# Attention and a mixture of experts on one core: some k loads leave the planner's estimate of transfers, and GpSimd's chores may follow each other after four steps, not five

## The chip, the cores and the metric

The kernel runs on one core of a Trainium2 chip. The metric is the device time of one execution in microseconds (us). The time before is the median of three runs. A profile of one execution stands beside them, with a trace of every instruction. Engines are named as in the profile: PE is TensorE's matmul, PEld its weight load, DVE is VectorE, ACT is ScalarE, POOL is GpSimd, SP is SyncE. A name with a small q behind it (SPq) is an engine's own queue of waits and DMA issues.

## The reference

Two blocks follow each other. The first is a lightning attention: for 4 batches and 8 heads, 768 positions of 64 channels, with a decay per head, and a state of 64 x 64 that is carried from block to block. Its output is laid out as 3072 tokens of 512 channels. The second is a mixture of four experts, each of two matrices with a ReLU between them, weighted by normalised probabilities.

```python
def _attn_ref(q, k, v, lam):            # q, k, v: (4, 8, 768, 64), block = 64
    ...
    for b in range(nb):
        sl = slice(b * block, (b + 1) * block)
        qb, kb, vb = (q[:, :, sl], k[:, :, sl], v[:, :, sl])
        intra = np.einsum('bhic,bhjc->bhij', qb, kb) * Dmask[None]
        intra = np.einsum('bhij,bhjd->bhid', intra, vb)
        inter = np.einsum('bhid,bhde->bhie', qb * lam_pow[None], kv_state)
        out[:, :, sl] = intra + inter
        kb_dec = kb * rev_pow[None]
        kv_state = lam_block[None, :, None, None] * kv_state + np.einsum('bhsd,bhse->bhde', kb_dec, vb)

def _moe_ref(x, domain_probs, w1, w2):  # x: (3072, 512), w1: (4, 512, 1024), w2: (4, 1024, 512)
    p = domain_probs / (domain_probs.sum(-1, keepdims=True) + 1e-09)
    for e in range(E):
        h = np.maximum(x @ w1[e], 0.0)
        out += p[:, e:e + 1] * (h @ w2[e])
```

All numbers are float32.

## The kernel before

**Tiling.** The 3072 tokens form three groups of 1024, and a group with one expert is a *unit*: twelve units, numbered 0 to 11. The products are done by a Strassen scheme with seven products (M1 to M7) in place of eight. For the products with the first weights (from unit 1 on), and from unit 5 on (`NEST`) for those with the second weights too, the scheme is nested: seven inner products in each of the seven. The operands of the nested products are sums and differences of weight blocks, called S1 to S4. They are made once on GpSimd, stored in device memory (`w1_ops`, `w2_ops`), and loaded from there again and again.

**The loop.** The main loop runs over the units (`at`), over the seven products (`i`), and over the eight entries of `order` (`x`). Each entry issues a few matmuls of the second product of this unit (L1234, from unit 5 on L1551) and of the first product of the next unit (L1175). One entry is a *step*; the planner's clock `now` goes up by one with each, so a unit has 56 steps. The order in which the program is written is the order in which every engine runs it; nothing is reordered later.

**Attention beside it.** Group 0's attention comes first. Groups 1 and 2 need 16 chunks of attention (n = 8 to 23), which run between the matmuls of units 0 to 4 at steps written out by hand (`AT`). From chunk 13 on (`comes_across`), q and k reach their transposed form through device memory and transposes on VectorE, and the untransposed k is loaded by itself, one DMA of 256 KB, in `load` (L174). GpSimd multiplies that k by the decay (`decayed`), and TensorE reads the product in `scores` (L761, L768) seven steps later.

**Weight loads.** `feed` (first weights, tile `ws_in`) and `feed3` (second weights in the nested form, tile `w2t`) load one product ahead, that is eight steps. Where the operands that they read were made by GpSimd, they call `until`, which forces chores out until the store of that operand has been issued. All of these loads, and nearly all stores, are issued by SyncE, in order.

**The planner.** GpSimd's preparations wait in a list, `chores`. After each step `pump` may hand out the first of them. It keeps estimates, in steps: `busy` (when GpSimd will be done), `moved` (when the transfers issued so far will have passed), `asked` (when SyncE will have issued them) and `free` (before which no further chore is begun). `send` is the helper that issues a DMA and adds it to the estimates:

```python
n = 4 * min(packet(out), packet(in_))
moved[0] = max(moved[0], now[0]) + 4 * math.prod(out.shape) / n * (9 + n / 25) / 16 / 1714
if by is None:
    asked[0] = max(asked[0], now[0]) + 0.27
```

A chore begins only if `free` has passed, `moved` and `asked` lie less than four steps ahead (`FULL`), and, from unit 4 on, GpSimd is not booked beyond the next step. Stores of what GpSimd made wait in `queue` until their estimated time, or until a chore begins, and are then issued. From unit 5 on (`spare` is set), at least five steps pass between two chores as long as more than 13 are left, and seven after that. In a chore of `prepare_w2_ops`, `ready` makes four inner operands by four subtractions (`inner_w2`) and books their store; `total` makes one of the sums S1, S2, S4. From unit 5 on it is second weights that are prepared in this way, M3 of expert 0 among them, which unit 7 needs for its second product.

Of the kernel before, what the change touches and what calls it, by code (L numbers as in the profile page):

```python
# [21 lines left out]
def kernel(  # L22
# [30 lines left out]
    nc = tc.nc  # L53

    B, H, S, D = q.shape
# [45 lines left out]
    def packet(ap):  # L101
        n, step = 1, 1
        for stride, size in reversed(ap.ap[1:]):
            if stride != step or size == 1 and stride != 1:
                break
            n, step = n * size, step * size
        return n

    def send(out, in_, by=None):
# [4 lines that stand above are left out]
        (by or nc.sync).dma_start(out=out, in_=in_)  # L114
# [13 lines left out]
    now, busy, free, filled, moved, asked, spare = [0], [0.0], [0.0], [0.0], [0.0], [0.0], []  # L128
# [21 lines left out]
    def where(n):  # L150
        g, x = divmod(n, CPG)
        return (x // 4, x % 4) if g == 0 else (2 * g + x // 2 % 2, 2 * (x // 4) + x % 2)
# [7 lines left out]
    def load(n, names="qkv"):  # L160

        c, b = where(n)
        for name in names:
            x = ({"k": acc_tile, "v": w2_tile} if n < CPG else {}).get(name, small)(f"{name}n")
            src = {"q": q, "k": k, "v": v}[name][b, :, c * C:(c + 1) * C, :]
            if name == "v":
                to, of = x[:].rearrange("p (h d) -> p h d", d=D), src.rearrange("h p d -> p h d")
                for h in (slice(0, 4), slice(4, 8)) if n < CPG else (slice(0, 8),):
                    send(out=to[:, h], in_=of[:, h], by=nc.scalar if n == 0 and h.start else None)
            else:  # L170
                to, of = x[:].rearrange("p (i r d) -> p i r d", r=2, d=D), src.rearrange("(r i) p d -> p i r d", r=2)
                if comes_across(n):
                    to = x[:].rearrange("p (r i d) -> p i r d", r=2, d=D)
                    send(out=x[:].rearrange("p (h d) -> p h d", d=D), in_=src.rearrange("h p d -> p h d"))  # L174
                else:
                    for r in range(2):
                        by = nc.scalar if n == 0 and r == 1 else nc.sync
                        by.dma_start(out=to[:, :, r], in_=of[:, :, r])
                nat[n, name] = to
                continue  # L180
            nat[n, name] = x[:].rearrange("p (h d) -> p h d", d=D)
# [13 lines left out]
    chores, queue, late, results, made = [], [], [], [], set()  # L195
# [8 lines left out]
    def all_added(still=None):  # L204
        while adds and (still is None or adds[0][0] < still):
            adds.pop(0)[1]()

    def pump(pace=1.0, force=False):
        all_added(None if force else now[0])
        while results:  # L210
            results.pop(0)()
        while late and (force or late[0][0] <= now[0]):
            late.pop(0)[1]()
        begins = chores and (
            force or free[0] <= now[0] and max(moved[0], asked[0]) < now[0] + FULL and not resting[0]
            and not (packed and busy[0] > now[0] + 1)
        )
        while queue and (force or queue[0][0] <= now[0] or begins and len(queue) > LEFT):
            queue.pop(0)[1]()
        if begins:  # L220
            begin = free[0] = max(free[0], now[0] - 1)
            was = max(busy[0], now[0])
            chores.pop(0)()
            free[0] = max(free[0], begin + max(pace * (busy[0] - was), (5 if len(chores) > 13 else 7) if spare else 1))

    def pause(n):
        def step():
# [4 lines left out]
    def until(what):  # L232
        while what not in made:
            pump(force=True)
# [271 lines left out]
    def comes_across(n):  # L506
        return n >= FIRST_ACROSS
# [11 lines left out]
    def load_more(n):  # L519
        if not comes_across(n):  # L520
            load(n, "qk")
        else:
            trickle(sum(x <= rank[where(n)[1]] for x, _ in pieces))
            load_across(n)
            load(n, "k")

    first = small("zeros")
    zeros = first[:, 0:P]
    nc.vector.memset(zeros, 0.0)
    load(0)  # L530
    load(1)
    raw_w1(0, "A11", 0)
# [32 lines left out]
    for r in range(2):  # L565
        for ac in range(NHP):
            h = 4 * r + ac
            nc.vector.tensor_tensor_scan(
                out=s_decay[:, r, ac], data0=lam_bc[:, h:h + 1].to_broadcast([P, BL]), data1=blk_ident,
# [10 lines left out]
    for ac in range(NHP):  # L580
        nc.vector.tensor_tensor_scan(
            out=q_decay[:, ac], data0=lam_q[:, ac:ac + 1].to_broadcast([P, BL]), data1=zeros[:, 0:BL],
# [549 lines left out]
    def first_product(g, e, m, blocks, tags):  # L1132

        while (g, e, m) not in fed:
            pump(force=True)
# [635 lines left out]
    for f in (  # L1771
        (ts[0], lambda: warm(2)), (ss[0],), (ts[1], lambda: warm(1)), (vs[0], loads(4, 5)), (ss[1], loads("A21", 6)),
        (vs[1], loads("A22", 7)), (ts[2],), (m1[0],), (ss[2],), (m1[2],),
        (vs[2],), (ts[3],), (h2[0][0],), (ss[3],), (ts[4],), (h2[0][1],),
        (vs[3],), (h2[2][0],), (ss[4],), (ts[5],), (h2[2][1], sum_first("S3", "A11", "A21")),
        (vs[4],), (h1[1][0],), (ss[5],), (ts[6], sum_first("S1", "A21", "A22", ALU.add)), (h1[1][1],),
        (vs[5],), (h1[3][0],), (ss[6],), (ts[7], load_probs), (h1[3][1], sum_first("S2", "S1", "A11")),
        (vs[6],), (h2[1][0], sum_x(0)), (ss[7],), (h2[1][1], sum_first("S4", "A12", "S2")),
        (begin_chores, m2[3]), (vs[7],), (sum_x(1), quarter_5(0)), (quarter_5(2),),
    ):  # L1780
        for work in f:
            work()
        now[0] += 1
        pump()
# [66 lines left out]
    for at, (g, e) in enumerate(units):  # L1851
# [14 lines left out]
        for i in range(7):  # L1866
# [8 lines left out]
            if nests and i == 2:  # L1875
                nc.scalar.dma_start(
                    out=gate_bc, in_=gate_rows[ahead[0] - 1, :, ahead[1]].partition_broadcast(P),
# [121 lines left out]
```

## Time and profile before

| | us |
|---|---|
| median of three runs | 1152.47 |
| the three runs | 1149.34, 1152.47, 1153.88 |
| the profiled execution | 1149.36 |
| its span, from first to last instruction | 1147.6 |
| TensorE busy in the span | 1134.2 |
| VectorE, GpSimd, ScalarE busy | 765.9, 762.9, 381.4 |

The mean clock that TensorE was granted is 0.996 of full speed. The profile's page gives shares, the costliest groups and the DMA issues; further views give the waits of an engine, the chain of work that ended last, the instructions in order of time, and stretches of the span with the busy time of each engine. A busy time of PE counts matmuls whose ends are modelled. A wait is put down to what came last.

### The profile page before, as it was taken

Reading aid. Unit: us, or ns where it says so; the run is one execution under the profiler, and the core shown is the slowest. Engines: PE = TensorE matmul, PEld = TensorE weight load, DVE = VectorE, ACT = ScalarE, POOL = GpSimd, SP = SyncE. Lnnn points to the kernel's source line nnn. Section 1 sums busy time; section 2 is a strip of 40 time slices with the busy share of each in tenths; the row PEclk is TensorE's granted clock in tenths of the full one; section 3 lists DMA queues with packets and bytes.
Section 4 is the critical chain, followed back from the end, with each engine's and each line's share of the span. In section 5 each row is a group of like instructions: output and inputs, shape, how many; then the busy total and the mean of one; then the engine's idle time right before and its main releaser. Section 6 shows DMA issues by size and latency. Waiting matters only on the chain.

```text
span 1147.6 us, 22118 instructions
## 1 busy us (share of the span) xinstructions
PE 1134.2 (99%) x7991; PEld 990.9 (86%) x7991; DVE 765.9 (67%) x1472; ACT 381.4 (33%) x770; POOL 762.9 (66%) x730
## 2 busy tenths in 40 slices
PE   8999999999999999999999999989999999999998
PEld 7888888888888888888888888868888888888887
DVE  4576776587577658737665576758767566776785
ACT  3425123112212311322353443344345442342332
POOL 2738148555743697547676995994896983873885
PEclk9999999999999999999999999989999999999999
DMA  8786888899789999778558677975669767657552
GB/s 199 176 276 190 204 230 256 280 327 297 244 284 311 289 296 307 246 235 297 176 174 266 208 249 222 298 253 182 189 205 291 227 192 200 194 162 211 174 193 74
DMA packets 322748, 266.34 MB, mean 232 GB/s; under 512 B 150160, under 2 KB 266064, under 8 KB 322640
## 3 DMA queue, kind: packets, MB, share of 16 engines
q1 hardware_dynamic: 287440, 257.61, 72.5%
q10 hardware_dynamic: 35168, 7.31, 3.5%
q8 instruction: 64, 1.05, 0.4%
q14 instruction: 44, 0.36, 0.1%
q0 software_dynamic: 32, 0.00, 0.0%
HBM read 197.19 MB, written 73.43 MB: 236 GB/s over the span
## 4 chain that ended last, share of the span: by engine, by line
PE 97%; DVE 1%; DMA 1%; issue 0%; ACT 0%; SPq 0%; DVEq 0%; POOLq 0%; ACTq 0%
PE pg L1175 41%; PE pq L1551 25%; PE q L1234 21%; PE pM L1693 2%; PE pc L1693 2%; PE op L824 1%; PE sp L761 1%; PE op L842 1%; PE sp L768 1%; PE pM L1418 1%; PE pg L1551 1%; PE qp L727 1%; PE kp L727 0%; DMA w2t<-w_ops 0%; DMA decay<-in_lam_dram 0%
## 5 line engine op out<-in xcount | busy, mean ns | idle before, releaser
L1175 PE MATMUL pg<-xs,ws_in 128*128 128x256 f32 x1960 | 471.2, 380 | 0.1
L1175 PEld LDWEIGHTS pg<-xs,ws_in 128*128 128x128 f32 x1960 | 372.1, 190 | 53.2 <-DVE m L117 2.5
L117 DVE TENSOR_TENSOR m<-pg,m 128x512 f32<-128x512 f32 x374 | 255.6, 686 | 93.1 <-PE pg L1175 81.0
L1234 PE MATMUL q<-w2t,m 128*128 128x256 f32 x1120 | 265.5, 380 | 0.0
L1234 PEld LDWEIGHTS q<-w2t,m 128*128 128x128 f32 x1120 | 211.7, 190 | 29.0
L117 DVE TENSOR_TENSOR sums<-pq,sums 128x256 f32<-128x256 f32 x272 | 113.2, 421 | 98.5 <-PE pq L1551 85.8
L1551 PE MATMUL pq<-acc,w2t 128*128 128x256 f32 x688 | 170.1, 380 | 0.0
L117 POOL TENSOR_TENSOR m<-m,decay 128x512 f32<-128x512 f32 x91 | 114.2, 1273 | 79.5 <-ACT m L1192 56.4
L1551 PEld LDWEIGHTS pq<-acc,w2t 128*128 128x128 f32 x688 | 131.2, 191 | 18.2
L1192 ACT ACTIVATE m<-m 128x512 f32<-128x512 f32 x99 | 62.4, 630 | 191.3 <-DVE m L117 191.1
L1252 DVE SCALAR_TENSOR_TENSOR acc<-q,gate,acc 128x256 f32<-128x256 f32 x108 | 52.1, 483 | 80.5 <-PE q L1234 79.7
L1188 ACT COPY m<-pg 128x512 f32<-128x512 f32 x88 | 51.6, 586 | 130.9 <-PE pg L1175 115.4
L117 DVE TENSOR_TENSOR m<-m,m 128x512 f32<-128x512 f32 x108 | 88.0, 815 | 6.5 <-ACT m L1158 6.5
L117 POOL TENSOR_TENSOR acc<-hT,hT 128x512 f32<-128x512 f32 x56 | 70.4, 1272 | 22.1 <-PE pq L1551 13.6
L1152 ACT COPY pg<-m 128x512 f32<-128x512 f32 x77 | 45.4, 590 | 110.8 <-DVE m L117 103.6
L117 POOL TENSOR_TENSOR acc<-hT,acc 128x512 f32<-128x512 f32 x56 | 71.2, 1271 | 7.3 <-PE pq L1551 3.6
L1551 PE MATMUL pq<-hT,w2t 128*128 128x256 f32 x288 | 70.0, 379 | 0.0
L117 POOL TENSOR_TENSOR kn<-kn,decay 128x512 f32<-128x512 f32 x16 | 18.4, 1148 | 65.2 <-DMA kn<-in_k_dram 31.3
L1551 PE MATMUL pq<-m,w2t 128*128 128x256 f32 x228 | 56.4, 384 | 5.2 <-DMA w2t<-w_ops 5.2
L1551 PEld LDWEIGHTS pq<-hT,w2t 128*128 128x128 f32 x288 | 54.7, 190 | 7.4
L117 POOL TENSOR_TENSOR w2o<-w2b 128x512 f32<-128x512 f32 x26 | 33.7, 1319 | 41.2 <-DMA w2b<-in_moe_w_dram 36.6
L1156 ACT COPY m<-pg 128x512 f32<-128x512 f32 x44 | 25.8, 586 | 91.0 <-PE pg L1175 85.1
(157 smaller groups left out, 1457.1 us busy)
## 6 DMA issues: line engine op xcount, KB each, us to landing
ws_in<-w_ops SPq DMA_DIRECT2D x40, 512.0 KB, 4.7
w2t<-w_ops SPq DMA_DIRECT2D x72, 256.0 KB, 3.1
ws_in<-w_ops SPq DMA_DIRECT2D x60, 256.0 KB, 3.7
ws_in<-w_ops SPq DMA_DIRECT2D x40, 384.0 KB, 4.2
w2b<-in_moe_w_dram SPq DMA_DIRECT2D x56, 256.0 KB, 5.3
w_ops<-ops SPq DMA_DIRECT2D x28, 512.0 KB, 5.0
w_ops<-ops SPq DMA_DIRECT2D x54, 256.0 KB, 4.0
w2t<-w_ops SPq DMA_DIRECT2D x100, 128.0 KB, 2.9
```

Source lines behind the costliest of these rows:

```text
L117: eng.tensor_tensor(out=o, in0=a, in1=b, op=op)
L727: nc.tensor.transpose(out=x[:, ac * C:(ac + 1) * C], in_=y[:, ac].rearrange("p r d -> p (r d)"), identity=ident[:],)
L761: nc.tensor.matmul(out=sp[r][half[x], ac * BL:(ac + 1) * BL], lhsT=hc(kT)[half[r], ac, blk[x]], rhs=hc(qT)[half[r], ac, blk[x]], start=(ac ...
L1152: nc.scalar.copy(out=banks[tags[1]][:], in_=new["11"][:])
L1156: nc.scalar.copy(out=o[:], in_=p[:])
L1175: nc.tensor.matmul(out=p[:, j * 256:(j + 1) * 256], lhsT=ws[i][:, j * P:(j + 1) * P], rhs=xs[i], start=(fresh and j == 0), stop=True, skip ...
L1188: nc.scalar.copy(out=new[at][:], in_=p[:])
L1192: nc.scalar.activation(out=new[at][:], in_=new[at][:], func=AF.Relu)
L1234: nc.tensor.matmul(out=p[:, s * DH:(s + 1) * DH], lhsT=h[A_OF[m]][:, c * 256 + s * P:c * 256 + (s + 1) * P], rhs=fed2[g, e, m][uu][:, c], ...
L1252: nc.vector.scalar_tensor_tensor(out=o, in0=x, scalar=w, in1=o, op0=ALU.mult, op1=ALU.add)
L1551: nc.tensor.matmul(out=p[:, 0:256], lhsT=fed3[e, m, i][:, c * P:(c + 1) * P], rhs=b[B_OF[i]][:, c * 256:(c + 1) * 256], start=(fresh and c ...
L1693: nc.tensor.matmul(out=p[:, s * 256:(s + 1) * 256], lhsT=a[c][:, f:f + P], rhs=b[:, c, j * 256:(j + 1) * 256], start=(s == 0 and c == 0 an ...
```

## The change

There are two edits, both in the planner. In `load`, the k of a chunk from 13 on is no longer issued through `send` but by a plain DMA on SyncE, with the same source and the same target: the transfer stays as it is, and `moved` and `asked` do not count it. In `pump`, the least distance between two chores from unit 5 on, while over 13 are left, is four steps instead of five.

```diff
@@ -171,7 +171,7 @@ in load
                 if comes_across(n):
                     to = x[:].rearrange("p (r i d) -> p i r d", r=2, d=D)
-                    send(out=x[:].rearrange("p (h d) -> p h d", d=D), in_=src.rearrange("h p d -> p h d"))
+                    nc.sync.dma_start(out=x[:].rearrange("p (h d) -> p h d", d=D), in_=src.rearrange("h p d -> p h d"))
@@ -221,7 +221,7 @@ in pump
             chores.pop(0)()
-            free[0] = max(free[0], begin + max(pace * (busy[0] - was), (5 if len(chores) > 13 else 7) if spare else 1))
+            free[0] = max(free[0], begin + max(pace * (busy[0] - was), (4 if len(chores) > 13 else 7) if spare else 1))
```

## The prediction

> **What bounds the kernel now.** I read the page first: the share of each engine and the chain that ended last. Busy time, share of the span, instructions; then the chain by engine.
>
> ```profile
> span 1147.6 us, 22118 instructions
> PE 1134.2 (99%) x7991; PEld 990.9 (86%) x7991; DVE 765.9 (67%) x1472; ACT 381.4 (33%) x770; POOL 762.9 (66%) x730
> ...
> PE 97%; DVE 1%; DMA 1%; issue 0%; ACT 0%; SPq 0%; DVEq 0%; POOLq 0%; ACTq 0%
> ```
>
> TensorE is the bound, and the change touches none of its work. So the question is only where TensorE waits. The view of its waits names them all:
>
> ```profile
> PE pq L1551 <- DMA w2t<-w_ops: 5.2, 1, 5.2
> PE sp L768 <- issue: 1.4, 1, 1.4
> PE op L824 <- ACT kv L784: 1.1, 2, 1.0
> ...
> PE sp L768 <- POOL kd L117: 0.3, 1, 0.3
> ```
>
> One wait stands out: 5.2 us, once, for a load of second weights (w2t). The stretches show what it costs. Rows are from:to, length, then busy time and count of PE, PEld, DVE, ACT, POOL, the granted clock, the DMA share and GB/s; the first two are stretches of chunk work in units 1 to 4, and the next four are units 6 to 9.
>
> ```profile
> 284.00:382.50 98.50, 98.50 (x887) 86.31 (x878) 66.60 (x129) 22.64 (x51) 48.28 (x54) 1.00 0.90 281
> 382.50:481.00 98.50, 98.50 (x897) 86.32 (x896) 68.46 (x125) 23.33 (x52) 74.02 (x84) 1.00 0.93 291
> ...
> 664.30:749.30 85.00, 84.94 (x393) 74.31 (x393) 62.23 (x122) 32.95 (x61) 70.14 (x68) 1.00 0.81 255
> 749.30:842.30 93.00, 87.77 (x393) 76.34 (x393) 67.11 (x133) 35.24 (x64) 69.65 (x62) 0.96 0.64 205
> 842.30:927.00 84.70, 84.70 (x393) 74.36 (x393) 53.22 (x94) 41.71 (x86) 71.41 (x65) 1.00 0.80 249
> 927.00:1011.70 84.70, 84.70 (x393) 74.42 (x393) 60.08 (x113) 29.67 (x54) 55.22 (x45) 1.00 0.64 187
> ...
> 763.10:768.40 5.30, 0.08 (x1) 0.03 (x1) 0.50 (x1) 1.08 (x2) 5.22 (x5) 0.90 0.92 280
> 768.40:774.90 6.50, 6.50 (x17) 5.26 (x18) 2.04 (x4) 0.59 (x1) 4.79 (x5) 0.56 1.08 365
> ```
>
> Units 6 to 9 have 393 matmuls each, and TensorE is dense in three of them: 84.70 us in units 8 and 9, 85.00 in unit 6. Unit 7 takes 93.00, so 93.00 - 84.70 = 8.30 us are lost in it. The last two rows split that: TensorE stands still for 5.2 us, and then works for 6.5 us at a mean granted clock of 0.56. The chain in order of time has the pieces (start, length):
>
> ```profile
> 763.23 5.04 DMA w2t<-w_ops
> 768.40 3.75 PE pq L1551 x8
> 772.15 2.78 PE pg L1175 x8
> 774.93 1.73 PE pq L1551 x8
> ```
>
> Sixteen matmuls took 3.75 + 2.78 = 6.53 us where two full-speed groups of eight take 2 x 1.73 = 3.46: 3.07 more. With the wait, 5.23 from the timeline below, that is 8.30 again: two independent sums agree.
>
> Why was the load late? The timeline of TensorE, of GpSimd and of SyncE's queue just ahead of it:
>
> ```profile
> 761.29 1.89 PE L1175 MATMUL pg<-xs,ws_in 128*128 128x256 f32 x8
> 768.40 2.04 PE L1551 MATMUL pq<-m,w2t 128*128 128x256 f32 x4 [5.23 <-DMA w2t<-w_ops]
> ...
> 754.23 2.50 POOL L117 TENSOR_TENSOR w2o<-w2b,w2o 128x512 f32<-128x512 f32 x2
> 756.68 1.42 POOL L117 TENSOR_TENSOR ops<-w2o 128x256 f32<-128x256 f32 x2
> 758.17 0.73 POOL L117 TENSOR_TENSOR ops<-ops,w2o 128x256 f32<-128x256 f32 x1
> 758.98 0.72 POOL L117 TENSOR_TENSOR ops<-w2o,ops 128x256 f32<-128x256 f32 x1
> ...
> 748.98 11.07 SPq L114 DMA_DIRECT2D w_ops<-ops  x4
> 760.10 0.95 SPq L114 DMA_DIRECT2D w_ops<-w2o  x2
> 761.10 2.04 SPq L114 DMA_DIRECT2D w2b<-in_moe_w_dram  x4
> 763.23 1.40 SPq L114 DMA_DIRECT2D w2t<-w_ops  x3
> ```
>
> Unit 7 begins at 749.30. There the program asks for expert 0's operands M3 (`until` in `feed3`), which no chore has made yet, so it forces the remaining chores out at once. SyncE's queue is in order: the stores of M3 stand ahead of the loads that read them, and wait for GpSimd, which finishes the four subtractions at 758.98 + 0.72 = 759.70. Four issues of stores spread over 11.07 us; the load goes out at 763.23, about 14 us after it was wanted, and TensorE was ready for it at 761.29 + 1.89 = 763.18. All its 5.04 us lie bare.
>
> **The change part by part.** Neither edit adds or removes an instruction on an engine that computes. Both alter when the planner lets a chore go. I followed its counters (`now`, `free`, `moved`, `asked`) through the code; a step is one entry of `order`, 84.70 / 56 = 1.51 us in units 8 and 9. This is bookkeeping of the program, with no time of the chip in it:
>
> ```
>                                      before     changed
> chores left when unit 5 begins           35          30
> expert 0's M3 stored at step            449         426
> M3 first wanted at step                 449         449
> forced chores from unit 5 on              3           0
> ```
>
> The order of GpSimd's instructions in the changed program agrees: expert 0's last sum and the subtractions of M3 stand 27 rows earlier in its queue (row 383, not 410), and TensorE's order is the same in both.
>
> *The k loads.* Eleven loads of a chunk's k, 256 KB each, are no longer counted. Each had pushed `moved` by 1024 pieces x (9 + 256/25) / 16 / 1714 = 0.72 steps and `asked` by 0.27, both of which can hold a chore back. By unit 5 that frees five chores, worth 5 x 5 = 25 steps of the old pace. The loads themselves remain:
>
> ```profile
> kn<-in_k_dram SPq DMA_DIRECT2D x11, 256.0 KB, 4.9
> ...
> w2t<-w_ops SPq DMA_DIRECT2D x100, 128.0 KB, 2.9
> ```
>
> Their landing takes 4.9 us at the median. What it may cost: five chores with their transfers move into units 1 to 4, where the DMA share is already 0.90 and 0.93. From below nothing is to be gained there, since TensorE is busy 98.50 of 98.50 us. From above, one weight load that comes as late as the one shown costs 8.30. I take 0, because loads are issued a product (8 steps) ahead: in those stretches 8 x 98.50 / 56 = 14.1 us, against landings of 2.9 to 4.9 us at the median, which leaves over 9 us.
>
> *The pace.* From unit 5 a chore may follow after four steps, not five. Following the counters, unit 5 still gets ten chores (other gates hold too) and unit 6 eleven instead of ten; unit 7 falls from nine to seven. One chore of four subtractions is 1.42 + 0.73 + 0.72 = 2.87 us of GpSimd, so unit 6 rises from 70.14 to about 73.0 of 85 us. GpSimd also makes operands there that TensorE reads. From below 0, from above one chore's 2.87 us if TensorE stood right behind it; in the trace TensorE waits for GpSimd 0.3 us in all, so I take 0.
>
> *The wait.* M3 is stored 449 - 426 = 23 steps earlier, 23 x 1.51 = 34.8 us, and no store is forced at 749.30. The load for unit 7 then goes out at its turn, 8 steps = 12.1 us ahead of use, and lands in about 2.9. What is late next? By the counters nothing is forced until the end, and in the trace no other load holds TensorE over a microsecond once unit 0 has begun. So both halves go, the 5.23 and the 3.07.
>
> Sum: -8.30 + 0 + 0 = -8.30 us. On the profiled execution, 1149.36 us (span 1147.6 and 1.8 around it), that gives 1141.1. The runs lie at 1149.34, 1152.47 and 1153.88; the profiled one sits at the lowest, 3.11 under the median. I take the saving off the median: 1152.47 - 8.30 = 1144.2 us. Should those 3.11 be a longer form of the same stall, the result is 1141.1.
>
> [...] VectorE's subtractions from two buffers in SBUF run slower than those that read PSUM:
>
> ```profile
> L117 DVE TENSOR_TENSOR m<-pg,m 128x512 f32<-128x512 f32 x374 | 255.6, 686 | 93.1 <-PE pg L1175 81.0
> L117 DVE TENSOR_TENSOR m<-m,m 128x512 f32<-128x512 f32 x108 | 88.0, 815 | 6.5 <-ACT m L1158 6.5
> ```
>
> They take 815 ns against 686. The change moves GpSimd work into units 1 to 4, where they run; VectorE is busy only 66.60 and 68.46 of 98.50 us there and TensorE did not wait for it, so I count nothing. [...]
>
> **The rivals.**
>
> *Another load comes late (0.17).* The chores now meet the chunk loads that nobody counts, and one weight load of units 2 to 6 slips past its use. For it: the shares 0.90 and 0.93, and a queue in which one blocked store delays all behind it. Against: the 9 us of room. A wait like the old one without its slow clock gives back 5.23: 1152.47 - 8.30 + 5.23 = 1149.4. [...] Here one gap of 5.23 did bring the clock down, and no shorter one is seen.
>
> *Slower: keys late on GpSimd (0.06).* The chunks' k is scaled on GpSimd in its queue's order, for scores that TensorE runs seven steps later.
>
> ```profile
> POOL kn L117 <- DMA kn<-in_k_dram: 31.3, 5, 12.2
> ```
>
> GpSimd already waits here 31.3 us in five chunks. If a chore now stands ahead of the scaling in each of the eleven chunks and TensorE feels all of its 2.87 us, that is 31.6: 1152.47 - 8.30 + 31.6 = 1175.8. It decides from 8.30 + 5.76 = 14.1 us on, 1.28 per chunk. Against it: the seven steps are 12.3 us, and TensorE waited 0.3 us for this so far.
>
> *The change does not reach the wait (0.04).* The estimate was not what held the chores, M3 is still forced, and all stays at 1152.5. The counters (30 left, not 35) speak against it.
>
> [...]
>
> **How the numbers follow.** The forecast has 0.70, and 1144.2 is its time; its own range is 1141.0 (the lowest run less 8.30) to 1146.7. A difference of 0.5%, 5.76 us, is about what a measurement of this kernel can tell from no change: under 1146.7 is faster, over 1158.2 slower. Faster: 0.69 of the forecast and 0.04 of the late load, where it is short: 0.73. Slower: 0.06 + 0.03 = 0.09. The rest is 0.18. The range for 8 in 10 runs from 1140.5 to 1149.9: 0.5 beyond the forecast's lower end and the late load's 1149.4, which leaves out the slower cases, the unreached wait and a few long late loads.
>
> **What would show it.** Right: TensorE's waits have no w2t row; unit 7 takes 84.7 to 85.0 us with a clock of 1.00; the `w_ops<-ops` issues near 749 no longer spread over 11 us; units 1 to 6 keep their lengths; the span is near 1139.3. Wrong: a new row of TensorE waiting for ws_in, w2t or kd, a second clock dip, or a w2t row that remains.

## The result and the profile after

The changed kernel runs in 1142.28 us (median of six, 1141.44 to 1143.16); the kernel before, over six runs, in 1150.90 (1148.07 to 1154.38). The ratio is 0.9923 with a 95% interval of 0.9900 to 0.9945: a gain of 0.77%, clear of the 0.5% that the prediction set as its bound. The profiled execution took 1143.16 us, its span 1141.4.

First TensorE's waits after the change, each with its total, count and longest; these are all there are:

```profile
PE kp L727 <- DMA kn<-in_k_dram: 1.4, 4, 0.6
PE zp L550 <- DVE zeros L529: 1.1, 1, 1.1
PE pg L1175 <- DVE m L117: 1.0, 2, 0.6
PE op L824 <- ACT kv L784: 1.0, 1, 1.0
PE pc L1693 <- DVE xs L117: 0.7, 1, 0.7
PE sp L761 <- ACT kT L736: 0.2, 1, 0.2
PE pM L1693 <- DVE m L117: 0.2, 1, 0.2
```

The row for w2t is gone. Small ones for VectorE are new. Now the stretches, with the columns of the prediction: one of chunk work in units 1 to 4, then four that start where unit 6 did. In this execution unit 7 begins about 1.2 us later than in the one before, at 750.5.

```profile
284.00:382.50 98.50, 97.49 (x872) 85.02 (x862) 70.02 (x127) 22.54 (x50) 58.21 (x63) 1.00 0.92 286
...
664.30:749.30 85.00, 84.94 (x394) 74.31 (x393) 62.19 (x122) 32.61 (x60) 74.44 (x70) 1.00 0.82 265
749.30:834.00 84.70, 84.70 (x393) 74.08 (x392) 66.81 (x133) 35.30 (x65) 69.25 (x65) 1.00 0.69 216
834.00:918.70 84.70, 84.70 (x394) 74.41 (x393) 53.19 (x94) 41.72 (x86) 58.85 (x50) 1.00 0.72 221
918.70:1003.40 84.70, 84.70 (x393) 74.37 (x392) 60.04 (x113) 29.67 (x54) 55.24 (x45) 1.00 0.64 187
```

Every stretch of 84.70 us from 749.30 on holds about 393 matmuls at full clock, where those of unit 7 took 93.00: 8.30 less. Counted from the first matmul of unit 7 to the first of unit 8, it is 93.2 and 85.2 us. In units 1 to 4 TensorE now stands still for 1.0 us of one stretch. The two spans differ by 6.2 us only: of the 8.0 us from unit 7, about 1.3 are lost again around that standstill and 0.6 behind the last matmul. The profiled execution after is also the slowest of its six.

SyncE's queue where unit 7 begins:

```profile
747.71 0.90 SPq L114 DMA_DIRECT2D w2b<-in_moe_w_dram  x2
749.69 4.75 SPq L114 DMA_DIRECT2D w2t<-w_ops  x3
754.49 0.46 SPq L114 DMA_DIRECT2D ws_in<-w_ops  x1
```

No store stands ahead of the loads of w2t there. The first goes out at 749.69, not at 763.23.

### The profile page after: what moved, and what is told of

Its sections match the earlier page's. It is cut to its first block, busy times and chain, and to the rows that moved or that the text cites. A ratio compares the mean times of both kernels' runs of the same rounds, so it can differ in the third digit from the quotient of the medians.

```text
span 1141.4 us, 22113 instructions
## 1 busy us (share of the span) xinstructions
PE 1131.5 (99%) x7991; PEld 987.4 (87%) x7991; DVE 771.4 (68%) x1472; ACT 381.2 (33%) x770; POOL 764.5 (67%) x730
## 4 chain that ended last, share of the span: by engine, by line
PE 93%; SPq 4%; DMA 2%; DVE 1%; issue 1%; ACT 0%; DVEq 0%
PE pg L1175 40%; PE pq L1551 25%; PE q L1234 20%; SPq L114 3%; PE pc L1693 2%; SPq L178 1%; PE op L824 1%; PE op L842 1%; PE pM L1693 1%; PE sp L761 1%; PE sp L768 1%; PE pM L1418 1%; PE pg L1551 1%; DVE m L117 1%; DMA w2t<-w_sums 0%
## 5 line engine op out<-in xcount | busy, mean ns | idle before, releaser
L1175 PE MATMUL pg<-xs,ws_in 128*128 128x256 f32 x1960 | 470.3, 380 | 1.1 <-DVE m L117 1.0
L1175 PEld LDWEIGHTS pg<-xs,ws_in 128*128 128x128 f32 x1960 | 370.9, 190 | 54.6 <-DVE m L117 4.3
L117 DVE TENSOR_TENSOR m<-m,m 128x512 f32<-128x512 f32 x108 | 93.1, 862 | 6.5 <-ACT m L1158 6.5
```

The costliest lines, as they stand in the source:

```text
L117: eng.tensor_tensor(out=o, in0=a, in1=b, op=op)
L1175: nc.tensor.matmul(out=p[:, j * 256:(j + 1) * 256], lhsT=ws[i][:, j * P:(j + 1) * P], rhs=xs[i], start=(fresh and j == 0), stop=True, skip ...
```

## The experiments

**Each edit alone.** The k loads left out of the estimate, pace five:

```diff
-                    send(out=x[:].rearrange("p (h d) -> p h d", d=D), in_=src.rearrange("h p d -> p h d"))
+                    nc.sync.dma_start(out=x[:].rearrange("p (h d) -> p h d", d=D), in_=src.rearrange("h p d -> p h d"))
```

> The first edit alone: the eleven k loads leave the estimate, the pace stays at five. By the planner's counters 30 chores are left when unit 5 begins and M3 of expert 0 is stored at step 430, not forced. Theory (the load only has to be asked for in time): the wait on w2t and the slow clock behind it are gone, unit 7 takes about 84.9 us, and the time is that of the changed kernel within 1.5 us, 1141 to 1144 us; TensorE keeps the two short waits for VectorE near 329 and 340 us (together 1.3 us) that the changed kernel's profile shows. Rival (the pace carries the gain): the wait stays, time as before, 1149 to 1153 us.

Measured: 1141.75 us (1140.94 to 1142.36), ratio 0.9925 (0.9906 to 0.9944). And the pace alone, k loads counted:

```diff
-            ... (5 if len(chores) > 13 else 7) if spare else 1))
+            ... (4 if len(chores) > 13 else 7) if spare else 1))
```

> The second edit alone: pace of four, the k loads counted as before. By the counters 35 chores are left when unit 5 begins and M3 is stored at step 439, not forced. Theory (the load only has to be asked for in time): the wait is gone here too, unit 7 takes about 84.9 us. The two waits for VectorE near 329 and 340 us come from chores moved into unit 2, so they are absent, and the time is 1 to 1.5 us below the changed kernel's, about 1141 us. Rival (the k loads carry the gain): the wait stays, 1149 to 1153 us. Rival on the two VectorE waits (they are chance of one execution): they show here as well.

Measured: 1142.26 us (1141.30 to 1144.67), ratio 0.9929 (0.9909 to 0.9950). Neither profile has a w2t row among TensorE's waits. So each edit by itself removes the wait, and the two together bring no more than one: three medians within 0.6 us. Both rivals that gave the gain to one edit fall.

The smaller claims of the expectations fared worse. With the k edit alone one wait for VectorE shows, 0.2 us, not the two that were expected, though up to unit 5 its program is that of the changed kernel. With the pace alone the two waits are absent as expected, but the time is not lower than the changed kernel's. Its profile, of the slowest of its six runs (1144.67), shows something else:

```profile
366.01 0.65 PE L761 MATMUL sp<-qx,kx 64*64 64x64 f32 x32
369.65 0.68 PE L768 MATMUL sp<-vn,kn 64*64 64x64 f32 x16 [2.99 <-issue]
```

TensorE stands still 2.99 us before the second half of a chunk's scores, with no releaser found. More of that below.

**Is it the forcing, or the amount of work in front?** The k edit with a pace of six, so that M3's store is forced again, with less work in front of it:

```diff
-            ... (5 if len(chores) > 13 else 7) if spare else 1))
+            ... (6 if len(chores) > 13 else 7) if spare else 1))
```

> The first edit, with a pace of six. By the counters M3 is forced again at step 449, but its last sum was made earlier, so only one chore (four subtractions, 2.87 us of GpSimd) stands between the request and the store, not two and a block of older stores. Theory (what counts is how much GpSimd work stands ahead of the store, against 12.1 us of lead): the load goes out 3 to 6 us late, lands in time, no wait on w2t, 1141 to 1144 us. Rival (a forced chore is a stall by itself): a wait of 3 to 5 us and the slow clock come back, 1146 to 1151 us.

Measured: 1143.06 us (1140.84 to 1145.12), ratio 0.9936 (0.9915 to 0.9957). No wait on w2t. The last of M3's subtractions on GpSimd, then SyncE's queue:

```profile
746.44 0.73 POOL L117 TENSOR_TENSOR ops<-w2o,ops 128x256 f32<-128x256 f32 x1
...
749.88 0.85 SPq L114 DMA_DIRECT2D w_ops<-ops  x2
750.79 1.59 SPq L114 DMA_DIRECT2D w_ops<-w2o  x2
752.47 2.97 SPq L114 DMA_DIRECT2D w2b<-in_moe_w_dram  x4
756.06 1.51 SPq L114 DMA_DIRECT2D w2t<-w_ops  x3
```

Unit 7 begins at about 752.7 in this execution, as the start took longer. M3's subtractions had ended at 746.44 + 0.73 = 747.17: by the planner's counters their chore went out in its turn, at step 443, and only the store was forced at step 449. So not even the one chore that the expectation names stood in front. In front of the load, which goes out some 3.4 us after its turn, at 756.06, stand only the next chore's four loads of w2b, and TensorE does not notice. A forced request is no stall by itself: without GpSimd's work in front, the lead of 12.1 us absorbed the rest here. The other way round, the kernel before with a pace of six, so that more stands in front:

> The kernel before with a pace of six instead of five: the suspected cost made larger. By the planner's counters 35 chores are left when unit 5 begins, M3 of expert 0 is forced at step 449 with 18 left, and M1 of expert 0 (step 441) and M3 of expert 3 (step 393) are forced too. Theory (the bare time is the store's delay behind GpSimd beyond the 12.1 us of lead): more GpSimd work stands ahead of the forced stores, the wait for w2t grows from 5.2 to 9 to 14 us with the slow clock behind it, 1155 to 1162 us. Rival (one forced request costs what it costs, however many chores): 1149 to 1153 us as before.

Measured: 1157.76 us (1156.75 to 1161.48), ratio 1.0064 (1.0042 to 1.0086), slower. The wait has grown as the theory had it:

```profile
PE pq L1551 <- DMA w2t<-w_ops: 11.7, 1, 11.7
...
777.36 2.04 PE L1551 MATMUL pq<-m,w2t 128*128 128x256 f32 x4 [11.66 <-DMA w2t<-w_ops]
```

**The end of the queue in front of the load.** The kernel before, but a forced request ends at the store, so that the next chore's loads don't slip in ahead of w2t:

```diff
-    def pump(pace=1.0, force=False):
+    def pump(pace=1.0, force=False, what=None):
...
-        if begins:
+        if begins and what not in made:
...
-            pump(force=True)
+            pump(force=True, what=what if spare else None)
```

> The kernel before, with one difference: a forced request ends as soon as the operand is stored, so the chore behind it, whose four loads of w2b took 2.04 us of the queue just ahead of the late w2t load, goes out later. GpSimd's two chores still stand in front of the store. [...]

Measured: 1145.39 us (1142.80 to 1153.07, 12 runs), ratio 0.9963 (0.9945 to 0.9980). Queue, TensorE, and the two stretches:

```profile
749.11 11.04 SPq L114 DMA_DIRECT2D w_ops<-ops  x4
760.20 0.95 SPq L114 DMA_DIRECT2D w_ops<-w2o  x2
762.31 1.55 SPq L114 DMA_DIRECT2D w2t<-w_ops  x3
...
765.08 1.10 PE L1551 MATMUL pq<-m,w2t 128*128 128x256 f32 x4 [1.88 <-DMA w2t<-w_ops]
...
763.20:765.10 1.90, 0.02 (x2) 0.05 (x1) 0.38 (x1) 1.08 (x2) 1.82 (x3) 1.00 0.83 249
765.10:772.00 6.90, 6.90 (x32) 6.10 (x33) 3.65 (x8) 2.21 (x5) 6.74 (x6) 1.00 0.94 284
```

The stores still spread over 11.04 us behind GpSimd. The load goes out 0.9 us earlier only, but lands in 2.6 us instead of 5.04, with no other load just ahead of it. The wait is 1.88 us, within the author's estimate of 1 to 3 (from the 2.04 us that the four loads took of the queue, and a landing of 2.9 in place of 5.04), and the clock stays at 1.00. So in this execution 3.35 us of the wait and all 3.07 of the slow clock hung on four loads that nobody needed yet. The medians give them less: 1145.39 against 1150.13 for the runs of the kernel before that stood beside it, 4.7 us. A second profile was to show whether the clock falls in executions that take longer:

> The kernel whose forced request ends at the store, profiled a second time: its runs lie between 1142.8 and 1153.1 us. [...] Rival: the gap and the clock are as in the first profile, whatever the time.

It took 1143.31 us, with a wait of 2.0 us and no half clock: alike, and none of the executions of 1145 us or more was caught. The median of this kernel lies 3.6 us above that of the k edit alone, more than its wait, so in some executions more than the wait must be lost. The clock has a part in that. The mean granted clock of the twelve runs is 0.999 or 1.000 in the seven up to 1145.47 us, 0.994 to 0.998 in the five from 1146.26 on, and 0.003 of such a span is 3.4 us. At which place the clock fell in those five, no trace shows.

**What varies before?** The runs of the kernel before scatter over 10 us in all, 1147.05 to 1157.0. Two more profiles of it:

> The kernel before, unchanged, profiled a second time, to see what varies between its executions (1148.0 to 1156.7 us in the runs so far, against 1141.4 to 1143.2 for the changed kernel). Theory (the spread belongs to the wait and the clock behind it): the wait on w2t is there again, 4 to 7 us, and where this execution is slower than 1149.4 the extra lies in a longer wait or a longer half clock. Rival (the spread is elsewhere): wait and clock as in the first profile, and the difference lies before unit 1 or in waits with no releaser.

> The kernel before, unchanged, profiled a third time. As for the second: by the theory the wait on w2t shows again with 4 to 7 us, and its length and the half clock behind it explain the difference in time to the other profiles; by the rival they are alike and the difference lies elsewhere.

They took 1153.11 and 1153.52 us. The wait on w2t is there both times, 5.0 and 5.4 us, as in the first profile, and unit 7 takes 92.2 us by its matmuls, 1.0 less than in the first; the extra lies elsewhere. In the second, then in the third profile:

```profile
369.14 0.68 PE L768 MATMUL sp<-vn,kn 64*64 64x64 f32 x16 [2.05 <-issue]
...
367.98 1.12 PE L768 MATMUL sp<-vn,kn 64*64 64x64 f32 x16 [2.53 <-issue]
...
365.50:367.90 2.40, 0.00 (x0) 0.00 (x0) 0.00 (x0) 0.82 (x5) 0.00 (x0) 0.92 1.24 290
367.90:374.20 6.30, 6.22 (x28) 5.15 (x29) 2.05 (x6) 0.57 (x2) 2.89 (x4) 0.50 0.97 299
```

The theory put into words there falls, the rival holds: a second standstill, the same as with the pace alone, here with a half clock (a granted clock of 0.50) behind it. The 800 matmuls around it, TensorE's 3500th to 4300th, take 81.9 and 83.7 us, and 78.0 in the first profile. Less the 1.0 of unit 7, that is 2.9 of the 3.75 us by which the second profile is slower than the first, and all of the 4.16 of the third. The matmuls of L768 read a chunk's k and v. The k had been scaled 11 us earlier; the v is this DMA, in the third profile, in the first, and in the changed kernel (size, then us to landing, of the one v load issued between 355 and 366 us):

```profile
360.60 0.37 SPq L114 DMA_DIRECT2D vn<-in_v_dram  x1
vn<-in_v_dram SPq DMA_DIRECT2D x1, 256.0 KB, 7.3
...
358.08 0.72 SPq L114 DMA_DIRECT2D vn<-in_v_dram  x1
vn<-in_v_dram SPq DMA_DIRECT2D x1, 256.0 KB, 7.9
...
356.81 0.38 SPq L114 DMA_DIRECT2D vn<-in_v_dram  x1
vn<-in_v_dram SPq DMA_DIRECT2D x1, 256.0 KB, 7.1
```

In the third profile it lands at 360.60 + 7.3 = 367.9, and TensorE goes on at 367.98. In the first it landed at 358.08 + 7.9 = 366.0, when L768 began, at 366.04: no wait, but no room either. In the changed kernel it lands at 363.9, and L768 begins at 367.11: 3.2 us of room. Wherever the k loads are counted, a chore's six loads of w2b and two stores of sums go out just ahead of this v; with the k edit the loads and one of the stores come earlier. Of seven profiles with the k loads counted and this v at its old place four stand still here, 1.9 to 3.0 us; of three with the edit none does. Among the seven, as among the three, the programs are the same up to unit 5. Does this v make the spread before? The v moved from 8 to 11 steps ahead:

```diff
-    V_AHEAD = {CPG + 10: 8, CPG + 13: 10}
+    V_AHEAD = {CPG + 10: 11, CPG + 13: 10}
```

> The kernel before, with one number changed: the v of chunk 18 is loaded 11 steps ahead of its scores, not 8. In five profiles of kernels that count the k loads this v landed 0.1 us before TensorE went on with L768, after a standstill of 1.9 to 3.0 us near 366 us in four of them. Theory (this late v is what makes the slower half of the executions before): the standstill near 366 us and the half clock behind it are gone, the wait on w2t near 763 us stays; the runs draw together at 1147.5 to 1150 us, median about 1148.5, 1.5 to 2.5 us under the median before. Rival (the spread comes from the wait on w2t or from the start): median and spread as before, 1148 to 1154 us.

Measured: 1149.92 us (1147.20 to 1153.07, 12 runs), ratio 0.9989 (0.9971 to 1.0008). The standstill at L768 is gone in its profile, and the median stays. None of the twelve runs lies above 1153.07 us, where five of the seventeen of the kernel before beside it do; that hints at the late v in the slowest runs and shows no more. A shorter standstill has come just behind, the traffic being what it was:

```profile
368.91 1.13 PE L1175 MATMUL pg<-xs,ws_in 128*128 128x256 f32 x4 [0.75 <-DMA ws_in<-w_ops]
```

> The second edit alone (pace of four, k loads counted), with the v of chunk 18 loaded 11 steps ahead, not 8. Theory (the k edit saves the late v, the pace saves the late w2t, and each wait is a load of its own): neither standstill is left, 1140.5 to 1142.5 us, as with the k edit alone (median 1141.75), and 0.3 to 1.5 us under the pace alone (1142.26). Rival (the v load moves the delay to another load): a new wait of 1 to 3 us near 350 to 370 us, 1142 to 1145 us.

Measured: 1142.01 us (1139.33 to 1143.67), ratio 0.9910 (0.9883 to 0.9937): neither standstill is in the profile, and the median is 0.25 us under the pace alone, within the spread. So the late v is a second wait that the k edit takes away; what it is worth at the median can't be told from nought with these runs, and the spread before is explained only in the two profiles in which it was caught. Of the 43 runs of the kernel before that stood beside the experiments, the four slowest, 1154.86 us and more, are the four with the lowest mean clock, 0.994; where it fell in them is open.

The versions without the wait on w2t (both edits, either alone, the k edit with a pace of six, the pace with the earlier v) lie at 1141.75 to 1143.06 us; none is better than another by more than their spread.

## Why the prediction was right

The time forecast was 1144.2 us in a range of 1140.5 to 1149.9; 1142.28 came.

*The wait.* 5.23 us of standstill and 3.07 of slow clock were to go, and unit 7 to fall from 93.00 to 84.70. It did, within 0.3 us. The store made 23 steps earlier was the cause named; `k_pace6` and `pace6` bear it out from both sides, since the wait grows with GpSimd's work in front of the store, and none shows where that work is done and the load goes out 3.4 us late. What the prediction left out: the same forced request also began the next chore, whose loads stood in SyncE's queue between the store and w2t, and with their traffic the landing took 5.04 us, against 2.6 in `stop`. The size depends on the execution, too: unit 7 took 93.2 us in the first profile and 92.2 in the two others of the kernel before, so the saving was 8.3 or 7.3 us.

*The k loads, counted at 0.* The deciding reason, room of 9 us for loads a product ahead, held for the weights: no wait for ws_in or w2t came. But in the profile after the term was not 0: TensorE waited twice for VectorE beside the chores moved into units 1 to 4, 1.0 us in all. The chance of slower holds 0.03, the author's estimate, for TensorE held up behind VectorE beside those chores until the time is clearly longer; no run shows that, and 1.0 us of waits is what this profile showed in its place. Nor are these waits shown to be a steady price of the moved chores: `k_only` and `k_pace6`, with the same program up to unit 5, show 0.2 us and none, and `pace6` and `stop`, which move no chore there, 0.4 and 0.6. VectorE's rows, GpSimd's row for the same time, and TensorE's longer wait:

```profile
322.03 0.68 DVE L117 TENSOR_TENSOR m<-m,m 128x512 f32<-128x512 f32 x1
325.55 1.71 DVE L117 TENSOR_TENSOR m<-m,m 128x512 f32<-128x512 f32 x1
...
325.44 2.95 POOL L117 TENSOR_TENSOR w2o<-w2b 128x512 f32<-128x512 f32 x2 [11.39 <-DMA w2b<-in_moe_w_dram]
...
340.80 1.13 PE L1175 MATMUL pg<-xs,ws_in 128*128 128x256 f32 x4 [0.57 <-DVE m L117]
```

The same subtraction takes 0.68 us with GpSimd idle and 1.71 beside GpSimd's. The prediction's 815 against 686 ns comes apart in the same way in its own trace, `before`: of the 108 subtractions from two buffers in SBUF, the 47 with GpSimd idle have a median of 0.68 us, and the 61 beside it one of 0.80 and a longest of 1.79; those with an operand in PSUM have a median of 0.69 either way. What holds the longer ones up is not shown. In the other direction the term could be a gain, which the prediction's bound "from below nothing" excluded: the late v, 3.9 and 5.7 us in the two profiles that caught it. The trace showed no wait for it in that execution, but it showed the v landing when it was needed. Waits were read, room was not.

*The pace, counted at 0.* Right: with it alone, and with both, GpSimd never held TensorE in units 5 and 6. Beside the k edit it was not needed.

*The price of the late load as a rival.* It rested on the reading that no gap shorter than 5.23 us brought the clock down. That was misread: in the same trace gaps of 1.38 and 0.97 us, in the first chunks, did so at 16.4 us; the rows are in the last section. That a leftover wait costs itself alone, as 1149.4 has it, was the author's estimate, and no run shows it throughout: the clock stayed at 1.00 behind 1.88 us in `stop` and 2.99 us with the pace alone, and fell to 0.50 behind 2.05 us in the second profile before.

*The late load as a rival.* None came; the load of v, late at times before, was in time in the three profiles with the k edit.

*From the profile to the median.* The saving was taken off the median of three runs, 1152.47. Over six runs the median before is 1150.90, and 1150.90 - 8.30 = 1142.6, a third of a microsecond from the result. So the forecast of 1144.2 was high mostly by the three runs it started from. That the sum itself meets so closely is in part luck: the saving varies by 1.0 us between executions, and what the late v and the waits for VectorE are worth at the median lies within the spread.

## What to carry to other kernels

SyncE's queue, which ran in order, turned a preparation that was forced out late into a wait of the load behind it: four issues of stores spread over 11.07 us, then 5.23 us of TensorE. Measure the lead of the load against the work that stands in front of its store, and see what else the forcing lets into the queue. Price a standstill of TensorE with the slow matmuls behind it: here 5.23 became 8.30 in one execution. And ask of each load how long before its use it landed, not only whether somebody waited in the one execution that was profiled.

## What the runs showed of the hardware

The clock fell after a gap of 2.05 us, and did not after one of 2.99. In the first profile before, two gaps of 1.38 and 0.97 us were followed by a half clock; in the second, a gap of 2.05 us was; with the pace alone, a gap of 2.99 us was not. Each time the stretch with the gap comes first:

```profile
13.00:16.40 3.40, 1.29 (x56) 1.08 (x56) 1.61 (x6) 0.37 (x1) 1.06 (x1) 1.00 0.78 214
16.40:19.80 3.40, 3.40 (x13) 3.02 (x14) 0.98 (x2) 1.95 (x6) 0.00 (x0) 0.50 0.75 193
...
366.90:369.10 2.20, 0.19 (x15) 0.05 (x4) 0.00 (x0) 1.07 (x5) 0.00 (x0) 1.00 1.20 300
371.00:374.20 3.20, 3.20 (x9) 2.57 (x8) 2.36 (x6) 0.97 (x2) 2.66 (x4) 0.50 0.98 287
...
366.50:369.60 3.10, 0.16 (x12) 0.02 (x4) 0.00 (x0) 1.04 (x5) 0.00 (x0) 1.00 1.22 292
369.60:376.00 6.40, 6.35 (x43) 5.64 (x44) 4.35 (x10) 1.51 (x3) 2.92 (x4) 1.00 1.02 327
```

The length of a gap alone does not sort these cases. Gaps of 1.88 us (`stop`) and 2.99 us (the pace alone) were followed by a clock of 1.00; gaps of 2.05 and 2.53 us (the second and third profile before), 5.23 us (the first) and 11.66 us (`pace6`) by one of 0.50. In the first profile, at the late w2t, the clock was 1.00 from 763.2 to 767.2 us and 0.50 from 767.3 to 774.1: it fell before the gap ended at 768.40. Behind the gap of 2.05 us, TensorE's next eight matmuls of L1175 began at 369.75, and the clock is 0.50 from 371.0 us on. What else counts is open.
